# Linformer attention into a hardswish layer: eight first-layer groups by seven products, clips on ScalarE, a new order of steps

## The chip, the cores and the metric

The kernel runs on one core of one Trainium2 chip. The metric is the device time of one execution, in microseconds; the median of three runs before the change is 478.25 us (477.89 to 478.27). Less is better. The engines are called as the profile calls them: PE (matmuls), PEld (its weight loads), DVE (VectorE), ACT (ScalarE), POOL (GpSimd) and SP (SyncE, which here issues DMAs).

## The reference

For each of 8 batches with 8 heads, 1024 positions and head width 64, keys and values are first projected along the sequence to 64 rows; the softmax runs over those 64. The rows of all heads side by side (8192 x 512) go through two layers with a hardswish between them.

```python
k_proj = np.einsum('ks,bhsd->bhkd', E, k)
v_proj = np.einsum('ks,bhsd->bhkd', F, v)
attn = softmax(scale * np.matmul(q, k_proj.transpose(0, 1, 3, 2)))
x = np.matmul(attn, v_proj)          # then (b, s, h*d): 8192 x 512
h = x @ w_in                         # 512 -> 2048
g = h * np.clip(h + 3.0, 0.0, 6.0) / 6.0
out = g @ w_out                      # 2048 -> 512
```

## The kernel before

**Blocks.** A batch is cut into two blocks of 512 tokens (t = 0, 1), so there are 16. Per block the first layer makes `g` as 16 groups of 128 features by 512 tokens; a group L (`first_group`, L578) is 4 steps of depth, each two matmuls of 64 weight columns side by side (`in_columns`, L198 to L200). Its result in PSUM becomes `g` in `h_out` (L573): ACT makes `r = relu(h/6 + 0.5)` (L575), DVE `min(r, 1) * h` (L576).

**Second layer.** It is cut 2 x 2 x 2 and done with seven products instead of eight (the Winograd form of Strassen's method). `Sums` (L662) makes sums of quarters of `g`: `c` (written sc) on POOL, `a` in place and `b` (sb) on DVE, `d` (sd) on POOL in two halves; `a` goes in two calls, one inside the block and a(4,8), groups 4 to 7 with groups 12 to 15, at the start of the next; sums of `w_out` are made once. A `Pair` (L686) is one half of a block's rows: steps 7, 2, 5, 6, 1, 3, 4, each 8 times two matmuls with 256 columns. Products 2 and 5 share a PSUM tile `y`, and 6, 1, 3, 4 share a tile `x`: each adds on top of the last, and after each an engine takes the running value out (ACT by copy, DVE by subtraction), so the next product of the tile waits for that read.

**Four first-layer groups by seven products.** From batch 3 on, the last four groups (12 to 15) are done the same way by a `Quad` (L746): sums of `w_in` are made once (`sums_of_w_in`, L146), and two blocks of `w_in` are changed in place in batch 3 (L930). Four sums of x per block run on POOL (`Quad.sums`, L754). A step is two feature groups by two depths by 256 tokens. Its four results leave by `Quad.out` (L778): for three of them DVE subtracts, ACT makes the relu from SBUF (L784), POOL clips it by 1 (L789) and multiplies (L790); for the fourth, and for all in the very last block, ACT does the relu and DVE clips and multiplies at once (L787). The tiles `m7`, `m2`, `m5` have one buffer each.

**Attention** of the next batch is done beside the blocks. `projected` (L341) is 16 steps of matmuls, copies on ACT, and then two pieces by transposing DMAs on SP. `some_scores` (L349) fills four PSUM tiles for two pairs of heads, which ACT's `exps` free: the first pair's at once, the second's later. `add_up` (L305) sums exponentials on DVE; `sums_turned` (L315) and `spread_sums` (L325) turn and invert the sums on DVE and spread them by two and eight DMAs on SP. `some_values` (L355) fills four PSUM tiles that DVE multiplies into the next `xT` (L301). `load_next` and `behind_that` (L216, L256) load a later batch: POOL waits for the reader of the old data by a copy of one element, then issues the DMAs.

**Order.** Every engine runs its instructions in the order in which they are written. PE's order in a block is a list of steps (`ORDER` L850, `QUADS` L852): L0 is a group, A and B are the two pairs of the block before, N is this block's first pair, Q the quad. `plan` (L863 to L930) hangs acts of the attention on places such as (0, "L1"). `later` is a list of pieces popped one per step; `behind_steps` (L563) puts a piece off by some steps, and `step_done` (L566) counts them. PSUM has eight tiles: four `mm` (groups, and the tiles x) and four `at` (the tiles y, scores, values, projections).

Of the kernel before, what the change touches and what calls it, by code (L numbers as in the profile page):

```python
# [11 lines left out]
ALU = mybir.AluOpType  # L12


@with_exitstack
def kernel(
# [11 lines left out]
    nc = tc.nc  # L28
# [44 lines left out]

    def g_tile():
        return gpool.tile([P, FO, TOK], bf16, tag="g", name="g")
# [8 lines left out]
    ones = consts.tile([P, TOK], bf16, name="ones")  # L84
# [58 lines left out]
    v11, v12, v21, v22 = [w_in_sb[:, k:k + KX, f * P:(f + NQ) * P] for k in (0, KX) for f in (FO - 2 * NQ, FO - NQ)]  # L143
    v_sums = consts.tile([P, 3, KX, NQ * P], bf16, name="v_sums")

    def sums_of_w_in():  # L146
        add(v_sums[:, 0], v11, v21, nc.gpsimd)
        add(v_sums[:, 1], v11, v22, nc.gpsimd)
        sub(v_sums[:, 2], v11, v12, nc.gpsimd)
# [45 lines left out]

# [26 lines left out]

    class Attention:
        def __init__(self, b):
            self.b = b
            self.aT = {}
            self.parts = None
# [17 lines left out]
        def values_out(self, a):  # L245
            nc.scalar.copy(
                self.vp[a * KP:(a + 1) * KP], self.ps[KP:].rearrange("p (h d) -> p h d", d=D))
# [26 lines left out]
        def exps(self, j, tiles, when=lambda f: f()):  # L274
            self.aT[j] = aT = att.tile([P, 2, 2, HT], bf16, tag="aT", name="aT", bufs=KO + 1)
# [20 lines left out]
        def values(self, j, *allocs):  # L296
            return self.quads(lambda r, h: self.vp[r:r + KP, h, :], j, allocs)
# [6 lines left out]

        def add_up(self, *js):  # L305
            if self.parts is None:
                self.parts = att.tile([P, KO, 32], f32, tag="parts", name="parts", bufs=1)
            for j in js:
                nc.vector.tensor_reduce(out=self.parts[:, j], op=ALU.add, axis=mybir.AxisListType.X, apply_transpose=True,  # L309
                                        in_=self.aT[j].rearrange("p a r n -> p (a r n)").rearrange(  # L310
                                            "p (c i) -> p c i", i=32))

        def sums_turned(self):  # L315
            turned, other = [att.tile([P, KO * 32], f32, tag="turned", name="turned", bufs=2) for _ in range(2)]
# [23 lines left out]

# [5 lines left out]

# [47 lines left out]

    class First:
# [131 lines left out]
        def second_scores(self):  # L529
            for j in range(0, KO, 2):  # L530
                aT = att.tile([P, 2, 2, HT], bf16, tag="aT", name="aT", bufs=KO + 1)
# [20 lines left out]
    def h_part(h_ps, xT, t, fo, kos):  # L552
        for ko in kos:
# [19 lines left out]
    def h_out(h_ps, g, fo, when=now):  # L573
        r = rpool.tile([P, TOK], f32, tag="r", name="r")
        nc.scalar.activation(r, h_ps, AF.Relu, bias=0.5, scale=1.0 / 6.0)  # L575
        when(lambda: nc.vector.scalar_tensor_tensor(g[:, fo, :], r, 1.0, h_ps, op0=ALU.min, op1=ALU.mult))  # L576
# [84 lines left out]

    class Sums:  # L662


        def __init__(self, g):
            self.blocks = [g[:, k * KH:(k + 1) * KH, i * HT:(i + 1) * HT] for i in range(2) for k in range(2)]

        def c(self, engine=nc.gpsimd):
            self.sc = spool.tile([P, KH, HT], bf16, tag="sc", name="sc")
            add(self.sc, self.blocks[0], self.blocks[2], engine)  # L670

        def a(self, lo, hi):
            a21, a22 = [x[:, lo:hi] for x in self.blocks[2:]]
            sub(a21, a22, a21)

        def b(self):
            self.sb = spool.tile([P, KH, HT], bf16, tag="sb", name="sb")
            sub(self.sb, self.blocks[0], self.blocks[2])

        def d(self, engine=nc.gpsimd):  # L680
            self.sd = spool.tile([P, KH, HT], bf16, tag="sd", name="sd")
            for lo in range(0, KH, 4):
# [3 lines left out]
    class Pair:  # L686
# [6 lines left out]
        def product(self, n, ps, first=False):  # L693
# [4 lines left out]
                    7: lambda: (a22, w_sums[:, 0])}[n]()  # L698
            for k in range(KH):
# [46 lines left out]
    class Quad:  # L746

        def __init__(self, x, t, g, last):  # L750
            self.g, self.last = g, last
            self.blocks = [x[:, k:k + KX, t, i * HT:(i + 1) * HT] for i in range(2) for k in (0, KX)]

        def sums(self):  # L754
# [7 lines left out]

        def product(self, n, ps, first=False):
            a11, a12, a21, a22 = self.blocks
            x, w = {1: (self.xb, v_sums[:, 1]), 2: (a11, v_sums[:, 2]), 3: (self.xd, v22), 4: (a12, v21),
                    5: (self.xc, v12), 6: (self.xa, v11), 7: (a22, v_sums[:, 0])}[n]
# [6 lines left out]
        def copied(self, name):  # L773
            m = spool.tile([P, TOK], f32, tag="q" + name, name="q" + name)
            nc.scalar.copy(m, self.y)
            return m

        def out(self, h, i, j, engine=None):  # L778
            f = FO - 2 * NQ + j * NQ
            g = self.g[:, f:f + NQ, i * HT:(i + 1) * HT]  # L780

            def relu():
                r = rpool.tile([P, TOK], f32, tag="r", name="r")
                nc.scalar.activation(r, h, AF.Relu, bias=0.5, scale=1.0 / 6.0)  # L784
                r3, h3 = [v.rearrange("p (a n) -> p a n", a=NQ) for v in (r, h)]
                if self.last or engine is nc.vector:
                    behind_steps(1)(lambda: nc.vector.scalar_tensor_tensor(g, r3, 1.0, h3, op0=ALU.min, op1=ALU.mult))  # L787
                else:
                    nc.gpsimd.tensor_scalar(out=r, in0=r, scalar1=1.0, scalar2=None, op0=ALU.min)  # L789
                    nc.gpsimd.tensor_tensor(out=g, in0=r3, in1=h3, op=ALU.mult)  # L790

            behind_steps(2)(relu)

        def step(self, n):
            if n in (7, 2):
                self.y = pat()
            elif n == 6:
                self.x = pmm()
            self.product(n, self.y if n in (7, 2, 5) else self.x, n in (7, 2, 6))
            if n == 7:  # L800
                self.m7 = self.copied("m7")
            elif n == 2:
                self.m2 = self.copied("m2")
            elif n == 5:
                self.m5 = self.copied("m5")
            elif n == 6:
                sub(self.m7, self.m7, self.x)
                self.out(self.m7, 1, 0, nc.gpsimd)
            elif n == 1:
                sub(self.m5, self.m5, self.x)  # L810
                self.out(self.m5, 1, 1, nc.gpsimd)
            elif n == 3:
                sub(self.m2, self.x, self.m2)
                self.out(self.m2, 0, 1, nc.gpsimd)
            else:
                self.out(self.x, 0, 0, nc.vector)
# [15 lines left out]
    for what in "A2 A7 V0 B7 A5 V1 A6 R B2 A1 V2 B5 R A3 B6 V3 A4 B1 R".split():  # L832
# [11 lines left out]
        if what in added:  # L844
# [13 lines left out]
    for b in range(1, B):  # L858
# [18 lines left out]
        def spread(turned, inverted):  # L877
            at(turned, lambda: second.sums_turned())
            at(inverted, lambda: second.spread_sums())

        if b == 1:
            at((0, "B4"), sums_of_w_in)
            at((1, "L0"), add_up(1))
            at((0, "L14"), scores(0, 1))
            at((1, "L1"), scores(2, 3))
            at((1, "N2"), values(0))
            at((0, "L12"), second.load_next)
            at((0, "L14"), add_up(0))
            at((1, "L2"), add_up(2))
            at((1, "L3"), add_up(3))  # L890
            spread((1, "A1"), (1, "B2"))
            at((1, "B4"), values(3))
            at((0, "L6"), second.projected)
            at((1, "B3"), values(1))
            at((1, "B3"), values(2))
            at((1, "B4"), lambda: behind_that(second.recs[1][:1, 0, :1], 3, "q"))
        elif b == 2:
            at((0, "B4"), add_up(2))
            at((0, "B6"), add_up(0))
            at((0, "L0"), second.projected)  # L900
            at((0, "L9"), scores(0, 1))
            at((1, "B4"), values(3))
            at((1, "B1"), values(0))
            at((0, "A1"), second.load_next)
            spread((1, "A1"), (1, "B2"))
            at((0, "L14"), scores(2, 3))
            at((1, "L6"), third.projected)
            at((0, "N5"), add_up(1))
            at((1, "L1"), add_up(3))
            at((1, "L13"), values(2))  # L910
            at((1, "N5"), values(1))
        elif b + 1 < B:
            if b == 3:
                at((0, "start"), second.load_next)
            at((0, "L1"), scores(0, 1))
            at((0, "B7"), add_up(0))
            at((0, "A1"), scores(2, 3), add_up(1))
            at((0, "A3"), add_up(2))
            at((0, "A4"), add_up(3))
            spread((0, "B6"), (0, "B3"))  # L920
            if third:
                at((0, "B4"), lambda: third.projected(pause=False))
                if third.b + 1 < B:
                    at((1, "L7"), third.load_next)
        if 2 < b < B - 1:
            at((1, "L3"), values(0, 1))
            at((1, "L7"), values(2, 3))

        if b == 3:
            at((0, "A6"), lambda: add(v12, v12, v22, nc.gpsimd), lambda: sub(v21, v21, v22, nc.gpsimd))  # L930
# [5 lines left out]
        for t in range(NB):  # L936
# [4 lines left out]
            quads = (b, t) >= (3, 0)  # L941
            if quads:
                pairs["Q"] = Quad(xT, t, g, (b, t) == (B - 1, NB - 1))
            if not start:
                behind[0].sums.a(KH - left, KH)
            left = 2 * NQ if quads else 2
# [73 lines left out]
```

## Time and profile before

| what | value |
|---|---|
| runs | 477.89, 478.25, 478.27 us |
| profiled execution, first to last instruction | span 476.3 us |
| median of the runs less that span | 1.95 us |
| PE busy | 469.6 us, 99% of the span |
| DVE, POOL, ACT busy | 339.4, 306.1, 275.4 us |
| granted clock of PE | 1.000 |

Durations come from the profiled execution. The profile gives its span; its own time with what lies around the span is not listed, so the 1.95 us stand for that. "Busy" counts overlapping instructions once. A row of the page's groups names line, engine, operation, the tiles written and read, how often, then the busy time, the mean of one in ns, and the idle time before. PE's matmuls overlap, so a step's cost is read from the distance to the next step's start. In the waits, a line says who waited for whom, how long in all, how often, and the longest.

### The profile page before, as it was taken

What the parts mean: (1) busy time and instruction counts of PE and PEld (TensorE: products, weight loads), DVE (VectorE), ACT (ScalarE), POOL (GpSimd) and SP (SyncE); (2) the same over time, 40 slices, a digit from 0 to 9 for tenths busy, and PEclk for the clock granted to TensorE, in tenths of its full rate; (3) what the DMA queues carried; (4) which work ended last, traced back from release to release, by engine and by line L of the source; (5) the groups of instructions that cost most, each with busy time, mean ns of one, the idle gap of its engine ahead of it and who ended that gap; (6) DMA issues with size and microseconds to landing.
All of it is one profiled execution on the core that took longest, in us unless ns stands there. A gap on an engine that the chain in (4) does not pass through costs nothing.

```text
span 476.3 us, 14916 instructions
## 1 busy us (share of the span) xinstructions
PE 469.6 (99%) x6428; PEld 346.1 (73%) x6428; DVE 339.4 (71%) x542; ACT 275.4 (58%) x534; POOL 306.1 (64%) x207
## 2 busy tenths in 40 slices
PE   7999999999999999999999999999999999999997
PEld 4554567667677766787787878778687877878797
DVE  2583387688765958886778876887778897747574
ACT  3766478675455654656466565666457545546451
POOL 8634966153335232867897778887788587888820
DMA  9999989688999939996999196962931054111012
GB/s 166 198 200 207 240 146 207 124 144 149 238 180 156 214 100 200 200 206 157 192 165 171 48 228 136 211 126 89 205 101 47 36 125 136 45 47 45 33 59 90
DMA packets 84609, 68.65 MB, mean 144 GB/s; under 512 B 38336, under 2 KB 70592, under 8 KB 84544
## 3 DMA queue, kind: packets, MB, share of 16 engines
q0 software_dynamic: 33024, 29.36, 39.7%
q1 hardware_dynamic: 51152, 37.83, 33.1%
q8 instruction: 50, 0.82, 0.7%
q10 hardware_dynamic: 368, 0.52, 0.3%
q14 instruction: 15, 0.12, 0.1%
HBM read 71.83 MB, written 16.97 MB: 186 GB/s over the span
## 4 chain that ended last, share of the span: by engine, by line
PE 92%; DMA 3%; ACT 2%; POOL 1%; DVE 0%; issue 0%; POOLq 0%
PE mm L200 68%; PE at L200 21%; DMA w_in_sb<-in_moe_w_in_dram 2%; PE at L289 2%; DMA k<-in_k_dram 1%; PE at L268 1%; ACT aT L277 1%; POOL k L110 0%; POOL q L106 0%; PE at L459 0%; DVE parts L309 0%; ACT rec L212 0%; ACT rec L206 0%; ACT m L705 0%; PE at L439 0%
## 5 line engine op out<-in xcount | busy, mean ns | idle before, releaser
L200 PE MATMUL mm<-xT,w_in_sb 128*64 128x512 bf16 (+1 forms) x1808 | 221.8, 375 | 0.2
L576 DVE SCALAR_TENSOR_TENSOR g<-r,mm 128x512 bf16<-128x512 f32 x216 | 146.2, 681 | 70.7 <-ACT r L575 69.8
L575 ACT ACTIVATE r<-mm 128x512 f32<-128x512 f32 x216 | 128.3, 598 | 117.3 <-PE mm L200 111.1
L200 PEld LDWEIGHTS <-w_in_sb 128*64 128x64 bf16 x2048 | 117.0, 110 | 59.7 <-issue 3.3
L200 PEld LDWEIGHTS <-g 128*64 128x64 bf16 x2048 | 112.6, 110 | 24.0 <-issue 4.1
L139 POOL TENSOR_TENSOR sd<-g,sb 128x1024 bf16<-128x1024 bf16 x28 | 59.1, 2130 | 42.0 <-DVE sb L139 40.7
L136 POOL TENSOR_TENSOR sc<-g 128x2048 bf16<-128x2048 bf16 x14 | 57.0, 4072 | 44.7 <-DVE g L576 44.7
L200 PE MATMUL mm<-w_out_sb,g 128*64 128x256 bf16 (+1 forms) x1088 | 77.8, 286 | 0.0
L200 PE MATMUL at<-w_sums,g 128*64 128x256 bf16 x896 | 58.4, 273 | 0.3 <-DVE g L576 0.3
L789 POOL TENSOR_SCALAR r<-r 128x512 f32<-128x512 f32 x27 | 41.5, 1538 | 15.2 <-ACT r L784 15.2
L705 ACT COPY m<-at 128x256 f32<-128x256 f32 x84 | 31.4, 373 | 30.1 <-PE at L200 25.6
L790 POOL TENSOR_TENSOR g<-r,qm 128x512 bf16<-128x512 f32 x27 | 36.3, 1345 | 2.3
L301 DVE TENSOR_TENSOR xT<-at,rec 128x512 bf16<-128x512 f32 x54 | 34.9, 683 | 2.3 <-DMA rec<-turned_rows 1.6
L139 DVE TENSOR_TENSOR o_sb<-m,mm 128x256 f32<-128x256 f32 x60 | 24.8, 413 | 9.6 <-PE mm L200 7.3
L200 PE MATMUL mm<-w_out_sb,sd 128*64 128x256 bf16 x480 | 31.3, 273 | 0.0
L200 PE MATMUL mm<-w_sums,sb 128*64 128x256 bf16 x480 | 31.2, 273 | 0.0
L277 ACT ACTIVATE aT<-at 128x512 bf16<-128x512 f32 x52 | 29.6, 601 | 2.3 <-PE at L268 2.3
L309 DVE TRANSPOSE_TENSOR_REDUCE parts<-aT 128x32 f32<-128x1024 bf16 x24 | 29.7, 1236 | 0.3 <-ACT aT L277 0.3
L200 PEld LDWEIGHTS <-sd 128*64 128x64 bf16 x480 | 26.5, 110 | 3.9 <-issue 0.2
L200 PE MATMUL at<-w_out_sb,sc 128*64 128x256 bf16 x448 | 29.3, 273 | 0.0
L200 PEld LDWEIGHTS <-sc 128*64 128x64 bf16 x480 | 26.5, 110 | 3.8 <-issue 0.3
L200 PEld LDWEIGHTS <-sb 128*64 128x64 bf16 x480 | 26.2, 110 | 4.0 <-issue 1.6
(118 smaller groups left out, 496.3 us busy)
## 6 DMA issues: line engine op xcount, KB each, us to landing
out_dram<-o_sb SPq DMA_DIRECT2D x60, 256.0 KB, 4.2
rec<-turned_rows SPq DMA_DIRECT2D x48, 256.0 KB, 6.1
k<-in_k_dram POOLq DMA_DIRECT2D x7, 1024.0 KB, 11.4
v<-in_v_dram POOLq DMA_DIRECT2D x7, 1024.0 KB, 15.9
q<-in_q_dram POOLq DMA_DIRECT2D x7, 1024.0 KB, 21.0
w_in_sb<-in_moe_w_in_dram POOLq DMA_DIRECT2D x7, 256.0 KB, 9.9
w_out_sb<-in_moe_w_out_dram POOLq DMA_DIRECT2D x3, 512.0 KB, 14.2
k<-in_k_dram POOLq DMA_DIRECT2D x4, 256.0 KB, 6.0
```

The costliest lines, as they stand in the source:

```text
L136: engine.tensor_tensor(out=out, in0=x, in1=y, op=ALU.add)
L139: engine.tensor_tensor(out=out, in0=x, in1=y, op=ALU.subtract)
L200: nc.tensor.matmul(ps[lo:lo + width], stationary[:, lo:lo + width], moving, **flags)
L277: when(lambda r=r: nc.scalar.activation(aT[:, :, r, :], tiles[r].rearrange("p (a n) -> p a n", a=2), AF.Exp, scale=scale))
L289: nc.tensor.matmul(tiles[t][c:c + D], stationary(r, 2 * j + a), self.weights(j, a)[r:r + KP], start=True, stop=True)
L301: when(lambda t=t: nc.vector.tensor_mul(self.xT[:, j, t, :], av[t], rec[:, t]))
L309: nc.vector.tensor_reduce(out=self.parts[:, j], op=ALU.add, axis=mybir.AxisListType.X, apply_transpose=True, in_=self.aT[j].rearrange("p a ...
L575: nc.scalar.activation(r, h_ps, AF.Relu, bias=0.5, scale=1.0 / 6.0)
L576: when(lambda: nc.vector.scalar_tensor_tensor(g[:, fo, :], r, 1.0, h_ps, op0=ALU.min, op1=ALU.mult))
L705: self.copy(m, ps)
L789: nc.gpsimd.tensor_scalar(out=r, in0=r, scalar1=1.0, scalar2=None, op0=ALU.min)
L790: nc.gpsimd.tensor_tensor(out=g, in0=r3, in1=h3, op=ALU.mult)
```

## The change

Eight groups instead of four, 8 to 15, are done by seven products, as two quads: Q for groups 12 to 15 and R for 8 to 11. The list of steps is written anew, the sums `a` to `d` and the sums of x (`+a`, `+b`, `+c`, `+d`, `+x`) become entries of it, and the last batch has lists of its own. The sums of x are made once for both quads. The clip on POOL goes: ACT makes two relus, `relu(0.5 - h/6)` and of that `relu(1 - r)`, and POOL only multiplies. The relu of a quad's result still stands two steps behind, DVE's product three steps behind instead of one, and the product of a group one step behind. The plan of acts is a table; several acts are at other places. The tile `aT` has four buffers instead of five, and `ones` is narrower. The code also keeps records of what is written when, which issue no instruction.

```diff
-    QUADS = ("L0 A7 L1 A6 L2 B7 L3 A1 L4 B2 L5 A3 L6 B5 L7 A4 "
-             "L8 Q7 Q2 B6 L9 Q6 N2 Q5 B1 L10 Q1 B3 L11 Q3 N5 B4 Q4").split()
+ORDER_OF_QUADS = ('L0 R7 A7 L1 +b +x L2 L3 L4 +d L5 L6 B2 A6 R2 R6 L7 R5 B7 B5 A1 +c R1 Q7 B6 A3 R3 Q6 B1 A4 '
+                  'Q2 B3 N2 Q5 Q1 N5 +a R4 Q3 B4 Q4')
+ORDER_OF_LAST = (('R7 L0 +b +x L1 R2 L2 A7 A6 L3 L4 +d L5 L6 B2 R6 L7 R5 B7 B5 +c A1 Q7 R1 B6 A3 R3 Q6 B1 A4 '
+                  'Q2 B3 N2 Q5 Q1 N5 +a R4 Q3 B4 Q4'),
+                 ('L0 R7 +x A7 +b L1 L2 R2 L3 L4 L5 L6 B2 R6 A6 L7 R5 +d A1 B7 B5 Q7 R1 +c B6 A3 R3 Q6 B1 A4 '
+                  'Q2 B3 N2 Q5 Q1 N5 +a R4 Q3 B4 Q4'))
-    ORDER = ("L0 A7 L1 A6 L2 B7 L3 A1 L4 B2 L5 A3 L6 B5 L7 A4 "
-             "L8 L9 B6 L10 N2 L11 B1 L12 N5 L13 B3 L14 L15 B4").split()
+ORDER_OF_L = ('L0 A7 L1 A6 L2 B7 L3 A1 L4 L5 B2 A3 L6 B5 L7 A4 L8 L9 B6 L10 N2 B1 L11 L12 N5 L13 B3 L14 '
+              'L15 B4')
...
+PLANS = {
+    1: ('0.L6:P 0.L12:l 0.L14:S01,u0 0.B4:wQ,wR 1.L0:u1 1.L1:S23 1.L2:u2 1.L3:u3 1.A1:T 1.B2:I '
+        '1.B1:V0 1.B3:V1,V2 1.B4:V3,q'),
+    2: ('0.B4:u2 0.B6:u0 0.L0:P 0.L9:S01 1.B4:V3 1.B1:V0 0.L2:l 1.A1:T 1.B2:I 0.L14:S23 1.B2:p '
+        '0.N5:u1 1.B7:u3 1.B3:V2 1.N5:V1'),
+    3: ('0.L1:S01 0.Q2:u0 0.L5:S23,u1 0.B5:u2 0.A1:u3 0.Q2:T 0.N2:I 0.B4:p 1.Q1:m 1.L3:V01 1.B1:V23 '
+        '0.L3:l 0.L1:iR 0.L3:iQ'),
+    4: ('0.L1:S01 0.Q2:u0 0.L5:S23,u1 0.B5:u2 0.A1:u3 0.Q2:T 0.N2:I 0.B4:p 1.Q1:m 1.L3:V01 1.B1:V23'),
+}
+FIRST_QUADS = (3, 0)
+RELU_BEHIND = 2
+PRODUCT_BEHIND = 3
+L_BEHIND = 1
+LEFT = 4
...
+    quarters = {"Q": Quarter(FO - 2 * NQ), "R": Quarter(FO - 4 * NQ)}
...
-                nc.scalar.activation(r, h, AF.Relu, bias=0.5, scale=1.0 / 6.0)
...
-                    nc.gpsimd.tensor_scalar(out=r, in0=r, scalar1=1.0, scalar2=None, op0=ALU.min)
+                    nc.scalar.activation(r, h, AF.Relu, bias=0.5, scale=-1.0 / 6.0)
+                    nc.scalar.activation(r, r, AF.Relu, bias=1.0, scale=-1.0)
                     nc.gpsimd.tensor_tensor(out=g, in0=r3, in1=h3, op=ALU.mult)
```

In the table, S is `some_scores`, V `some_values`, u `add_up`, T `sums_turned`, I `spread_sums`, P and p `projected` of the next batch and the one after, l and m their `load_next`, q a load of queries, w the sums of `w_in` for a quad and i its in-place sums. Plan 4 holds for batches 4 to 6. Before, in batches 3 to 6, S01 stood at L1, u0 at B7, S23 and u1 at A1, u2 at A3, u3 at A4, T at B6, I at B3 and p at B4 of t=0; V01 stood at L3, V23 and m at L7 of t=1.

More of the change, by code (lines that the diff above doesn't have):

```diff
@@ L71, in pat, with wrote, there @@
         return ps_at.tile([P, TOK], f32, tag="at", name="at")
+    written = {}
     def g_tile():
-        return gpool.tile([P, FO, TOK], bf16, tag="g", name="g")
+        g = gpool.tile([P, FO, TOK], bf16, tag="g", name="g")
+        written[id(g)] = set()
+        return g
+    def wrote(g, i, fos):
+        written[id(g)].update((i, f) for f in fos)
+    def there(g, i, fos):
+        assert all((i, f) in written[id(g)] for f in fos), (i, fos)
     scratch = g_tile().rearrange("p f n -> p (f n)")
@@ L83 @@
     nc.vector.memset(wide, 1.0)
-    ones = consts.tile([P, TOK], bf16, name="ones")
+    ones = consts.tile([P, D], bf16, name="ones")
     nc.vector.memset(ones, 1.0)
@@ L142, with __init__, sums, in_place @@
     NQ, KX = 2, KO // 2
[L143 to L149, printed above, removed]
+    class Quarter:
+        def __init__(self, f):
+            self.f, self.summed, self.changed = f, False, False
+            self.v11, self.v12, self.v21, self.v22 = [
+                w_in_sb[:, k:k + KX, a * P:(a + NQ) * P] for k in (0, KX) for a in (f, f + NQ)]
+            self.v_sums = consts.tile([P, 3, KX, NQ * P], bf16, name="v_sums%d" % f)
+        def sums(self):
+            assert not self.summed
+            self.summed = True
+            add(self.v_sums[:, 0], self.v11, self.v21, nc.gpsimd)
+            add(self.v_sums[:, 1], self.v11, self.v22, nc.gpsimd)
+            sub(self.v_sums[:, 2], self.v11, self.v12, nc.gpsimd)
+        def in_place(self):
+            assert self.summed and not self.changed
+            self.changed = True
+            add(self.v12, self.v12, self.v22, nc.gpsimd)
+            sub(self.v21, self.v21, self.v22, nc.gpsimd)
+    quarters = {"Q": Quarter(FO - 2 * NQ), "R": Quarter(FO - 4 * NQ)}
     def sums_of_w_out():
@@ L245, in values_out @@
         def values_out(self, a):
+            self.halves.add(a)
             nc.scalar.copy(
@@ L552, in h_part @@
     def h_part(h_ps, xT, t, fo, kos):
+        assert not any(q.changed and q.f <= fo < q.f + 2 * NQ for q in quarters.values())
         for ko in kos:
@@ L575, in h_out, with product @@
         nc.scalar.activation(r, h_ps, AF.Relu, bias=0.5, scale=1.0 / 6.0)
-        when(lambda: nc.vector.scalar_tensor_tensor(g[:, fo, :], r, 1.0, h_ps, op0=ALU.min, op1=ALU.mult))
+        def product():
+            nc.vector.scalar_tensor_tensor(g[:, fo, :], r, 1.0, h_ps, op0=ALU.min, op1=ALU.mult)
+            for i in range(2):
+                wrote(g, i, [fo])
+        when(product)
     def first_group(xT, t, g, fo, when=now):
@@ L669, in c @@
             self.sc = spool.tile([P, KH, HT], bf16, tag="sc", name="sc")
+            for i in range(2):
+                there(self.g, i, range(KH))
+            assert not self.ready
             add(self.sc, self.blocks[0], self.blocks[2], engine)
@@ L875, in add_up @@
             return lambda: second.add_up(*js)
[L877 to L930, printed above, removed]
+        acts = {"P": lambda: second.projected(), "p": lambda: third and third.projected(pause=b < 3),
+                "l": lambda: second.load_next(), "m": lambda: third and third.b + 1 < B and third.load_next(),
+                "T": lambda: second.sums_turned(), "I": lambda: second.spread_sums(),
+                "q": lambda: behind_that(second.recs[1][:1, 0, :1], 3, "q")}
@@ new lines, in act @@
+        def act(what):
+            if what in acts:
+                return acts[what]
+            if what[0] == "w":
+                return quarters[what[1]].sums
+            if what[0] == "i":
+                return quarters[what[1]].in_place
+            return {"S": scores, "V": values, "u": add_up}[what[0]](*map(int, what[1:]))
+        for entry in PLANS.get(b, PLANS[4] if 3 < b < B - 1 else "").split():
+            t, place, what = entry.replace(":", ".").split(".")
+            at((int(t), place), *map(act, what.split(",")))
```

110 lines of the change are left out of this document (73 added, 37 removed).

## The prediction

> **What bounds the kernel now.** I read the page's busy shares first, then the waits, then the busy time of two blocks, then PE's timeline inside them.
>
> ```profile
> span 476.3 us, 14916 instructions
> ...
> PE 469.6 (99%) x6428; PEld 346.1 (73%) x6428; DVE 339.4 (71%) x542; ACT 275.4 (58%) x534; POOL 306.1 (64%) x207
> ```
>
> PE leads by far. The view of waits must say whether it works or waits:
>
> ```profile
> PE at L200 <- DVE g L576: 0.3, 1, 0.3
> ```
>
> In the products of both layers (line 200) PE waits for another engine once, for 0.3 us, while ACT's relus wait for PE 158 times, 111.1 us in all. Now two blocks of batch 5 (t=0 and t=1, from the start of L0 to the start of the next L0):
>
> ```profile
> 301.14:330.00 28.86, 28.86 (x428) 22.61 (x426) 23.88 (x36) 17.82 (x37) 23.03 (x15) 1.00 0.64 131
> 330.00:356.99 26.99, 26.99 (x396) 21.12 (x394) 19.77 (x33) 15.45 (x31) 20.49 (x13) 1.00 0.79 162
> ```
>
> Columns: stretch and length, then PE, PEld, DVE, ACT, POOL, the granted clock (1.00). PE is busy for all of it, so no stall is there to be removed. Time can come only from PE having less to do, and is lost by every new PE wait.
>
> **What the change is worth on PE.** PE's timeline in that stretch prices each step by the distance to the next start:
>
> ```profile
> 306.18 1.04 PE L200 MATMUL at<-w_sums,g 128*64 128x256 bf16 x16
> 307.05 1.03 PE L200 MATMUL mm<-xT,w_in_sb 128*64 128x512 bf16 x8
> 307.91 1.04 PE L200 MATMUL mm<-w_sums,sb 128*64 128x256 bf16 x16
> ...
> 319.89 0.60 PE L200 MATMUL mm<-xa,w_in_sb 128*64 128x256 bf16 x8
> 320.32 1.04 PE L200 MATMUL at<-w_sums,g 128*64 128x256 bf16 x16
> ```
>
> A pair's product takes 307.05 - 306.18 = 0.87 us, a group L 0.865, a seven-product step (Q6) 0.434. Four groups cost 4 x 0.865 = 3.46, the seven products in their place 7 x 0.434 = 3.04: 0.42 less per block. The row of x sums counts 10 blocks (xc x10), the ones from batch 3 on: **10 x 0.42 = 4.2 us** less PE work. Attention, pairs and tail keep their PE work.
>
> A rule speaks against this. The Trainium skill, "TensorE: Matmul & The Clock Gate", Back-to-back issue gap, says that in a stream of weight loads and matmuls the spacing is set by both, some 81 ns per matmul at 128 columns and 131 at 512. An estimate on a line between gives 98 at 256, so 56 x 98 - 32 x 131 ns = 1.3 us more per block. The trace disagrees: 8 matmuls of 256 columns in 0.434 us are 54 ns each, 8 of 512 in 0.865 are 108. I keep the rows; rival 4 holds the rest.
>
> **What the other engines get, per block.** The rows:
>
> ```profile
> L576 DVE SCALAR_TENSOR_TENSOR g<-r,mm 128x512 bf16<-128x512 f32 x216 | 146.2, 681 | 70.7 <-ACT r L575 69.8
> ...
> L789 POOL TENSOR_SCALAR r<-r 128x512 f32<-128x512 f32 x27 | 41.5, 1538 | 15.2 <-ACT r L784 15.2
> ...
> L784 ACT ACTIVATE r<-qm 128x512 f32<-128x512 f32 x30 | 19.0, 633 | 9.2 <-DVE qm L139 9.2
> ```
>
> - DVE: minus four L products (0.681), plus three subs (0.688) and one product (0.688): +0.03.
> - POOL: minus three clips (1.538), plus three products (1.345, L790's row): -0.6.
> - ACT: minus four relus (0.598), plus three copies (0.586), nine relus from SBUF (0.633) and one from PSUM (0.597): +5.7. It gets 23.5 of 28.4 us in t=0, 21.1 of 26.6 in t=1. The second relu reads the first's result; the trace has no such pair. Bounds for two: 2 x 0.49 (distance of two relus that follow at once) to 2 x 0.633 plus a gap; I take 1.2.
>
> No engine passes PE's sum. What decides is lateness inside the block.
>
> **A walk through block t=0** (batches 3 to 6), time 0 at L0, PE without stalls. Ends on PE: L1 3.0, scores 0 and 1 3.6, L5 7.1, scores 2 and 3 7.6, R6 11.1, L7 12.0, A1 15.0, R3 18.1, Q6 18.5, B1 19.4, Q2 20.7, B3 21.6, Q5 22.9, Q1 23.3, N5 24.2, R4 24.6, Q3 25.1, B4 25.9, projection 27.7, Q4 28.1.
>
> ACT, in written order: Q3's two relus (1.2) and Q4's one (0.5) of the block before end at 1.7; then, at 0.49 per 512 columns and 0.25 per 256, L0, R7's copy, A7's copy, L1, two exps, L2, exp, L3, exp: the last frees its score tile at 6.6, before scores 2 and 3 (7.1). It is level with PE by L7 (relu to 12.5; R6's two behind it to 13.7). POOL: x sums from 2.6, when Q3's product of the block before ends, 4 x 1.16 and, between them, DVE's sb (1.2): 8.4; sd 2 x 2.13: 12.7 (A3 needs it at 16.8); R6's product 13.7 to 15.0; sc 4.07: 19.0 (N5 needs it at 23.3); then R1 to 20.3, R3 to 21.6, Q6 to 22.9. Three places are tight:
>
> 1. Q2's copy on ACT (the one tile m2) waits for R3's product, 21.6, so ends at 22.2; Q5, at 22.4, adds into the same PSUM tile. Margin 0.2.
> 2. Q3 (24.6) adds into the tile that Q1's sub on DVE reads. DVE before it: Q6's and B1's subs to 19.8, add_up(0) (1.236) to 21.0, then sums_turned, B3's sub, the reciprocal (0.94), Q1's sub. Without contention sums_turned takes 0.30 + 2 x 0.22 + 2 x 0.28 = 1.3 and the sub ends at 24.1; with a wait of 0.4 for the rest of R3's product, 24.6: margin about 0.
> 3. In t=1, B2 at 7.9 needs a PSUM slot that DVE's first value product frees; before it DVE has Q4's product (to 1.7), a(4,8), L0, L1, sb (to 6.0), L2 and L3 (to 7.2), so 7.9. Margin 0.
>
> The lock is seen in these rows:
>
> ```profile
> 304.00 1.28 POOL L790 TENSOR_TENSOR g<-r,qm 128x512 bf16<-128x512 f32 x1
> ...
> 304.11 2.25 DVE L139 TENSOR_TENSOR sb<-g 128x2048 bf16<-128x2048 bf16 x1
> ...
> 317.21 4.07 POOL L136 TENSOR_TENSOR sc<-g 128x2048 bf16<-128x2048 bf16 x1 [1.78 <-DVE g L576]
> ...
> 319.91 1.45 DVE L321 COPY turned<-turned 32x128 f32<-32x128 f32 x1
> ```
>
> The copy (0.22 alone) ends at 321.36, just after sc (321.28); sb takes 2.25 where it takes 1.23 beside an idle POOL. The Trainium skill, "SBUF — State Buffer", Who interferes with whom, says the same: a DVE copy, or a DVE operation with two SBUF inputs, and a GpSimd operation block each other whole. By that rule the adds of sums_turned wait too; that is rival 2.
>
> The last batch has no attention beside it, its last block every product on DVE; the tail's first steps find a(4,8) as late as now (2.2 us after Q4, needed at 2.6): 0. In batches 1 and 2 L5 goes ahead of B2, value products and add_ups move by a few steps, and two quarters' sums take 3.5 us more of a POOL that then idles 9.4 us: 0, bounds -0.3 and +0.5. In batch 3 the second quarter's in-place sums add 2.3 us to POOL ahead of sd, which has 4 to spare. load_next goes from L7 to Q1 of t=1: mark and three issues, 0.2 + 2.7 us of POOL, now stand ahead of Q1's product; that ends at 26.9 of 26.3, and the next A7 starts 1.3 into its block: 0.7 left. Its loads (11 to 21 us to landing) have over 25 us. spread_sums goes from B3 to N2: SP issues two and eight DMAs from 24 on (7 us now), 6.1 us to landing, while the first value product comes 9 us later: 0.
>
> So the place costs: each of the tight ones between 0 and 1.25; I charge 0.1 in each of the eight blocks with attention. **Sum: -4.2 + 0.8 = -3.4.** The profiled execution's span becomes 476.3 - 3.4 = 472.9; the median of the runs stands 1.95 above the span, for what lies around it, which the change leaves: 478.25 - 3.4 = **474.8**.
>
> **Rivals.**
> 1. As forecast, 473.8 (place costs and batches 1 and 2 at their best) to 476.4: 60%. For: every step is at a row's price. Against: margins of 0 to 0.2.
> 2. sums_turned is blocked twice: POOL takes the lock after the first copy for Q6's product, and add, second copy and all behind come 1.3 later; Q1's sub ends at 25.9 and Q3 waits 1.25. In two to four of the blocks t=0 that is 2.5 to 5.0 more: 477.3 to 479.8. For: the rows of the lock. Against: the adds' rows (0.28) show no wait so far. 20%.
> 3. **Slower:** POOL's queue is late in every block: sc (4.07) stands ahead of R1, R3 and Q6, so if R6's product or sd ends a microsecond later, Q2's copy, Q5 and the end of the block go with it. Nine blocks have POOL products; at 0.75 each it is 6.8, so 480.8. It decides from 0.47 per block (4.2 / 9), when sc starts after 15.7. For: R6's two relus stand behind L7's on ACT. Against: POOL has 0.6 less to do. 14%.
> 4. The change doesn't do what it says: 56 weight loads where there were 32 (110 ns each, PEld up from 73%) eat the saved columns: 478.25 + 0.8 = 479.0. Against: Q6's 0.434. By the page's rule it would be 13 us more, 491; 2 of this rival's 6%.
>
> **How the numbers follow.** The measurement can tell about 0.2% (0.96 us) from no change. Faster: rival 1's 60, 8 of rival 2, 2 of rival 3: 70%. Same: 8, 2 and 4 of rival 4: 14%. Slower: 4, 10 and 2: 16%. The range runs from 473.8 to 478.9, and leaves out the end of rival 2 and nearly all of rival 3, some 19%. The likeliest case's own range is 473.8 to 476.4.
>
> **What would show it.** Right: 40 L groups gone (x1728 to x1408 matmuls), products at 0.434, two blocks together near 55.0 us instead of 55.85, PE without gaps. Wrong at place 1: PE waits for ACT's qm copy before Q5. At place 2: PE idle before Q3 with DVE qm named and long turned rows. Rival 3: the copy of m2 waits for POOL g in every block, t=1 too. Rival 4: a Q step above 0.45 us. I am wrong if PE shows more than 3 us of new waits that none of these places holds.

## The result, and the profile after

The changed kernel takes 483.87 us (median of four runs, 483.5 to 487.03) where the kernel before takes 478.1 on the same chip: ratio 1.0133 [1.0103, 1.0162]. It is 1.3% slower. One of the four runs, the one of 487.03 us, had a granted clock of 0.993; by the medians alone the loss is 1.2%. The prediction said 474.8 and put 478.9 as its upper end, so it missed the direction too. The profiled run took 483.7 us, with a span of 481.9; the span before was 476.3, so the step to explain is +5.6 us.

The page of the changed kernel, its span and busy shares:

```profile
span 481.9 us, 15515 instructions
...
PE 467.6 (97%) x6668; PEld 361.4 (75%) x6668; DVE 343.6 (71%) x545; ACT 320.0 (66%) x618; POOL 310.8 (64%) x212
```

PE was busy for 99% of the span and is now busy for 97%: it has less to do in a longer time. The view of waits, three of PE's lines in the two layers (who waits for whom, total, times, longest):

```profile
PE mm L251 <- DVE qm L176: 3.4, 4, 1.0
PE mm L251 <- DVE g L628: 1.8, 3, 0.6
...
PE at L251 <- ACT qm L848: 0.8, 1, 0.8
```

Before there was one such line, of 0.3 us; one of that size is there after too. (Line 251 is the old line 200, 628 the old 576, 176 the old 139; 373, 374 and 379 are the old 321, 322 and 327.) Batch 5, cut at the starts of L0, in the columns used for it before:

```profile
304.86:334.23 29.37, 28.59 (x452) 23.84 (x450) 24.16 (x36) 23.76 (x48) 22.57 (x15) 1.00 0.75 143
334.23:362.15 27.92, 27.16 (x421) 22.71 (x419) 20.08 (x33) 19.27 (x38) 19.80 (x13) 1.00 0.64 152
```

The batch takes 57.29 us where it took 55.89 by the same cuts (301.15 to 357.04), and the length of each half is now above PE's busy time: 0.78 and 0.76 us of hard idle time, at an undisturbed clock.

The steps themselves cost what was foreseen. PE's timeline of the changed kernel in batch 4:

```profile
265.49 0.60 PE L251 MATMUL mm<-xd,w_in_sb 128*64 128x256 bf16 x8
265.93 0.60 PE L251 MATMUL mm<-xa,w_in_sb 128*64 128x256 bf16 x8
266.36 1.04 PE L251 MATMUL mm<-w_sums,sb 128*64 128x256 bf16 x16
```

Two steps of a quad take 0.44 and 0.43 us, start to start. So some 4.2 us of PE work did go. PE's busy time, down by only 2.0 us, is no measure of it: the run with one quad below, which has the PE work of the kernel before, shows 473.1 us of it against 469.6. Against the 4.2 stand 9.7 us of waits from batch 3 on, where the kernel before has 0.5: -4.2 + 9.2 is 5.0, beside 5.6; the other 0.6 was not traced. Where they lie, from the starts of PE's steps against the time that their columns take: before Q3 in t=0, 1.19 in batch 3 and 0.95 in each of batches 4 to 6 (4.0); in t=1 of batches 3 to 5, 0.77 before L6 and 0.31 before B2 (3.2), and 0.2 before B2 in batch 6; before Q5 in batch 3, 0.97; the last 1.3 is in pieces of at most 0.22, mostly 0.15 before Q4. By length, batch 3 gains 2.60 us, batches 4 and 5 some 1.4 each, batch 6 0.67, and the rest changes by less than 0.4 each.

**Before Q3** (place 2). The timeline of batch 4, t=0, of all engines; the row of POOL counts three products, and the bracket on PE's row is its wait:

```profile
267.13 3.75 POOL L870 TENSOR_TENSOR g<-r,qm 128x512 bf16<-128x512 f32 x3
...
269.40 0.33 DVE L373 COPY turned<-turned 32x128 f32<-32x128 f32 x1
...
269.77 1.26 DVE L374 TENSOR_TENSOR inv<-turned 32x128 f32<-32x128 f32 x1
...
271.04 0.22 DVE L373 COPY turned<-turned 32x128 f32<-32x128 f32 x1
...
271.95 0.93 DVE L379 RECIPROCAL inv<-inv 64x128 f32<-64x128 f32 x1
...
272.81 0.62 DVE L176 TENSOR_TENSOR qm<-qm,mm 128x512 f32<-128x512 f32 x1
...
273.48 0.63 PE L251 MATMUL mm<-xd,w_in_sb 128*64 128x256 bf16 x8 [0.79 <-DVE qm L176]
```

Q1's product left PE at about 271.4. Its subtraction starts at 272.81, because DVE has `sums_turned` and the reciprocal in front of it, and the first add of `sums_turned` takes 1.26 us where it takes 0.28: it ends 0.15 us after POOL's row does (270.88). Such a hold of a DVE instruction by one of POOL's is called the lock here. Q3 needs the tile at 272.5 and gets it at 273.48.

**Before L6 and B2** (place 3). Batch 4, t=1, whose L0 starts at 276.95:

```profile
280.90 1.64 ACT L625 ACTIVATE r<-mm 128x512 f32<-128x512 f32 x3
281.54 0.69 DVE L628 SCALAR_TENSOR_TENSOR g<-r,mm 128x512 bf16<-128x512 f32 x1 [1.23 <-ACT r L625]
...
282.04 1.15 POOL L176 TENSOR_TENSOR xd<-xT,xb 128x512 bf16<-128x512 bf16 x1
282.14 2.13 DVE L176 TENSOR_TENSOR sb<-g 128x2048 bf16<-128x2048 bf16 x1
...
284.19 1.27 DVE L628 SCALAR_TENSOR_TENSOR g<-r,mm 128x512 bf16<-128x512 f32 x2
...
284.92 1.05 PE L251 MATMUL mm<-xT,w_in_sb 128*64 128x512 bf16 x8 [0.60 <-DVE g L628]
285.39 0.68 DVE L353 TENSOR_TENSOR xT<-at,rec 128x512 bf16<-128x512 f32 x1
...
286.12 1.06 PE L251 MATMUL at<-w_sums,g 128*64 128x256 bf16 x16
```

ACT comes late to L1's relu, DVE idles for 1.23 us and then begins sb, which takes 2.13 instead of 1.23 because POOL's last sum of x runs beside its start. The products of L2 and L3 wait behind sb with two PSUM tiles in their hands, so L6 finds none; and B2's tile comes free only after the multiplication at 285.39.

**Before Q5** (place 1), in batch 3 alone, where POOL has the loads and the in-place sums of `w_in` besides:

```profile
209.64 3.72 POOL L870 TENSOR_TENSOR g<-r,qm 128x512 bf16<-128x512 f32 x3
...
210.95 2.50 DVE L373 COPY turned<-turned 32x128 f32<-32x128 f32 x1
...
212.17 0.58 ACT L848 COPY qm<-at 128x512 f32<-128x512 f32 x1 [1.03 <-POOL g L870]
...
212.81 0.63 PE L251 MATMUL at<-xc,w_in_sb 128*64 128x256 bf16 x8 [0.81 <-ACT qm L848]
```

ACT's copy waits for R3's product and Q5 for the copy. The DVE row is met again below.

### The profile page after: what moved, and what is told of

Same layout as the page of the kernel before. It is cut to its first block, busy times and chain, and to the rows that moved or that the text cites. A ratio compares the mean times of both kernels' runs of the same rounds, so it can differ in the third digit from the quotient of the medians.

```text
span 481.9 us, 15515 instructions
## 1 busy us (share of the span) xinstructions
PE 467.6 (97%) x6668; PEld 361.4 (75%) x6668; DVE 343.6 (71%) x545; ACT 320.0 (66%) x618; POOL 310.8 (64%) x212
## 4 chain that ended last, share of the span: by engine, by line
PE 82%; DVE 8%; ACT 5%; issue 3%; DMA 1%; POOL 0%; DVEq 0%; POOLq 0%
PE mm L251 57%; PE at L251 20%; PE at L340 1%; DMA k<-in_k_dram 1%; PE at L319 1%; DVE parts L361 1%; DVE qm L176 1%; DVE g L628 1%; ACT aT L328 1%; DVE turned L373 1%; DVE inv L374 1%; DVE inv L379 1%; ACT r L625 1%; ACT vp L297 1%; DVE o_sb L176 1%
## 5 line engine op out<-in xcount | busy, mean ns | idle before, releaser
L251 PE MATMUL mm<-xT,w_in_sb 128*64 128x512 bf16 (+1 forms) x1568 | 180.5, 369 | 1.9 <-DVE g L628 1.8
L251 PEld LDWEIGHTS <-w_in_sb 128*64 128x64 bf16 x2048 | 119.5, 110 | 66.0 <-issue 14.1
L628 DVE SCALAR_TENSOR_TENSOR g<-r,mm 128x512 bf16<-128x512 f32 x176 | 117.1, 680 | 47.5 <-ACT r L625 46.8
L625 ACT ACTIVATE r<-mm 128x512 f32<-128x512 f32 x176 | 103.8, 600 | 65.7 <-PE mm L251 63.0
L870 POOL TENSOR_TENSOR g<-r,qm 128x512 bf16<-128x512 f32 x54 | 68.1, 1276 | 48.8 <-ACT r L869 37.1
L868 ACT ACTIVATE r<-qm 128x512 f32<-128x512 f32 x54 | 34.0, 629 | 14.1 <-DVE qm L176 14.0
L848 ACT COPY qm<-at 128x512 f32<-128x512 f32 x60 | 35.0, 583 | 12.5 <-PE at L251 7.6
L869 ACT ACTIVATE r<-r 128x512 f32<-128x512 f32 x54 | 34.0, 630 | 1.7
L176 DVE TENSOR_TENSOR qm<-qm,mm 128x512 f32<-128x512 f32 x40 | 26.9, 673 | 8.6 <-ACT qm L848 4.1
```

What stands on the lines that cost most here:

```text
L176: engine.tensor_tensor(out=out, in0=x, in1=y, op=ALU.subtract)
L251: nc.tensor.matmul(ps[lo:lo + width], stationary[:, lo:lo + width], moving, **flags)
L848: nc.scalar.copy(m, ps)
L868: nc.scalar.activation(r, h, AF.Relu, bias=0.5, scale=-1.0 / 6.0)
L869: nc.scalar.activation(r, r, AF.Relu, bias=1.0, scale=-1.0)
```

## The experiments

The working theory was that three independent causes share the waits: the reciprocal and the lock before Q3, sb ahead of the value products in t=1, and POOL's queue in batch 3. The main rival was that the work of the second quad (ACT's double relus, POOL's products) fills the engines, whatever the order. All edits are to the changed kernel unless said otherwise. The kernel before measured 478.2 to 478.6 us beside them.

### One act moved at a time

**sums_turned and the reciprocal behind Q1**, so that Q1's subtraction comes first:

```diff
-0.Q2:T 0.N2:I
+0.Q1:T,I
```

> The changed kernel, with sums_turned and spread_sums of batches 3 to 6 moved from Q2 and N2 to behind Q1, where POOL is idle for some 4 us. Theory (DVE's turn of the sums is blocked by POOL's products and holds up Q1's sub, so PE waits 0.95 us before Q3 in each of four blocks t=0): these waits go, 483.8 - 3.8 = 480.0, within 0.6. Rival (ACT has too much to do with two relus for each clip, and every wait is a late relu): the waits stay, 483.5 to 484.

Measured 487.5 us, ratio 1.0172 [1.0142, 1.0203]: a miss. The waits before Q3 are gone, as foreseen, and larger ones stand before Q4: 1.2 us in batches 3 to 5 and 2.9 in batch 6 (2.73 of it shown as idle). Q3's own subtraction now stands behind everything that was moved, and behind `a`. DVE in batch 4:

```profile
273.15 0.21 DVE L373 COPY turned<-turned 32x128 f32<-32x128 f32 x1
273.40 0.28 DVE L374 TENSOR_TENSOR inv<-turned 32x128 f32<-32x128 f32 x1
...
274.27 0.94 DVE L379 RECIPROCAL inv<-inv 64x128 f32<-64x128 f32 x1
275.14 1.51 DVE L176 TENSOR_TENSOR g<-g 128x1024 bf16<-128x1024 bf16 x1
276.57 0.67 DVE L176 TENSOR_TENSOR qm<-mm,qm 128x512 f32<-128x512 f32 x1
```

The last row is the subtraction that Q4 waits for. The first two show what `sums_turned` costs when POOL has no row beside it: 0.21 and 0.28. In batches 3 to 5 the projection's matmuls (1.7 us) hide part of the queue; batch 6 has no projection.

**b behind L3**, so that the products of L2 and L3 and the first value product are not behind it:

```diff
-L0 R7 A7 L1 +b +x L2 L3 L4 +d
+L0 R7 A7 L1 +x L2 L3 +b L4 +d
```

> The changed kernel, with +b moved from behind L1 to behind L3 in the list of quads, so that DVE makes the products of L2 and L3 and the first value product before sb. Theory (sb, stretched to 2.1 us by POOL's sums of x, stands ahead of the products that free the PSUM slots for L6 and B2 in t=1): PE's waits before L6 (0.88) and B2 (0.42) go in three blocks, 483.8 - 3.9 = 479.9, within 0.7. Rival (the slots are late because ACT's relus are late): L6 still waits 0.5 or more, 482 to 483.8.

Measured 481.15 us, ratio 1.0054 [1.0039, 1.0068]. The waits before L6 and B2 are gone, sb takes 1.22 us there and meets no POOL row; the waits before Q3 stay (1.20 and three of 0.95). The time is 0.5 us above the theory's range: the expectation's 0.88 and 0.42 were too high, as the waits before L6 and B2 are 0.77 and 0.31, 3.2 in three blocks instead of 3.9. The move gave 2.7 of them.

**Both:**

> Both moves together. Theory: the two waits are independent and add up, 483.8 - 7.7 = 476.1, within 0.8, so below the 478.1 of the kernel before. Rival (PE then waits for something else that comes 1 us later, since ACT, DVE and POOL are all nearly full): half of it or less, 479.5 or more.

Measured 486.46 us, 1.0153 [1.0135, 1.0171]. That is far above the theory's 476.1, and the two do not add up: the spans would give 485.8 + 478.9 - 481.9 = 482.8 us, and this run has 484.5. The first one's loss before Q4 stays, and in t=1 of batches 3 to 5, where the waits before L6 and B2 are gone, R2 now waits 0.56 us and Q5 0.25, as the rival had it.

**add_up(0) earlier**, which takes 1.24 us out of DVE's queue ahead of `sums_turned`:

```diff
-0.Q2:u0
+0.R6:u0
```

> The changed kernel, with add_up(0) moved from Q2 to behind R6, where DVE is idle, so that sums_turned starts 1.2 us earlier but in the same company: three products on POOL without a gap. Theory (the copies and adds of sums_turned are kept out until POOL's row of products ends): sums_turned ends at most 0.4 us earlier and Q3 still waits 0.6 or more in each of four blocks, 482.2 to 483.8. Rival (DVE's queue is merely 1 us too long there, whatever POOL does): the waits go, 480.0.

Measured 483.47 us, 1.0093 [1.0072, 1.0115], so almost nothing against 483.87, and inside the theory's 482.2 to 483.8. `sums_turned` starts 0.8 us sooner and loses most of it again: the wait before Q3 falls from 0.95 to 0.70 us in batches 4 to 6. DVE in batch 4 of this run:

```profile
268.60 0.38 DVE L373 COPY turned<-turned 32x128 f32<-32x128 f32 x1
269.01 1.27 DVE L374 TENSOR_TENSOR inv<-turned 32x128 f32<-32x128 f32 x1
270.29 1.21 DVE L373 COPY turned<-turned 32x128 f32<-32x128 f32 x1
```

Two of its four small instructions are now held for a product of POOL's row each, instead of one. That is the lock: a shorter queue would have brought the whole 0.8.

### Who pays: the order or the second quad

**The new order with one quad**: groups 8 to 11 are computed as groups again, where R's seven steps stood.

```diff
-L0 R7 A7 ... B2 A6 R2 R6 L7 R5 B7 B5 A1 +c R1 Q7 B6 A3 R3 Q6 ... N5 +a R4 Q3 B4 Q4
+L0 L8 A7 ... B2 A6 L9 L7 L10 B7 B5 A1 +c L11 Q7 B6 A3 Q6 ... N5 +a Q3 B4 Q4
```

> The changed kernel's new order and plan, but groups 8 to 11 as groups again (L8 to L11 stand where R's seven steps stood, 4 x 0.865 us on PE instead of 7 x 0.434): the order alone, without the second quad. PE's work is that of the kernel before. My theory: the waits of t=1 (first relus behind the sum b on DVE, 1.3 us in each of batches 3 to 5) belong to the order and stay, 3.9 us; the waits before Q3 come from sums_turned meeting POOL's row of products of both quads, and with R's products gone they mostly go (0 to 1 us left). So 478.5 + 3.9 + 0.5 = 482.9 us (482.0 to 483.8). Rival A: all new waits come with the second quad's work on ACT and POOL: 478.5 (477.9 to 479.2). Rival B: the order alone makes the waits before Q3 too: 486.5 (485.5 to 487.5).

Measured 487.13 us, 1.0182 [1.0168, 1.0196]. Rival B's 486.5 is met, and my theory fell: I had given the waits before Q3 to the row of products of two quads, and they are there with one. Batch 4 of this run:

```profile
269.49 0.68 DVE L373 COPY turned<-turned 32x128 f32<-32x128 f32 x1
...
271.41 0.93 DVE L379 RECIPROCAL inv<-inv 64x128 f32<-64x128 f32 x1
...
272.26 0.62 DVE L176 TENSOR_TENSOR qm<-qm,mm 128x512 f32<-128x512 f32 x1
...
272.94 0.63 PE L251 MATMUL mm<-xd,w_in_sb 128*64 128x256 bf16 x8 [0.64 <-DVE qm L176]
```

The lock takes 0.46 here (0.68 against 0.22) instead of 1.0, but R4, which gave Q3 0.43 us more time, is not there either. What both kernels share is the reciprocal right in front of the subtraction, with little between Q1 and Q3. So the spans split the result: the new order with one quad costs 485.4 - 476.3 = 9.1 us, and the second quad within it brings 485.4 - 481.9 = 3.5 us back, of the 4.2 foreseen. The main rival, that the second quad's work makes the waits whatever the order, is out as the main cause. The waits of the two runs, 9.1 and 9.7 us, are not all the same ones, though: with one quad those before L6 are only 0.27, and 0.25 before Q3 in each t=1 of batches 3 to 6 and 1.8 before groups of batch 7 are its own.

**The reciprocal alone moved**, from N2 to Q1, with `sums_turned` left where it is:

```diff
-0.Q2:T 0.N2:I
+0.Q2:T 0.Q1:I
```

> The changed kernel with one edit: the reciprocal and the spreading stand behind Q1 instead of N2 (b stays behind L1, a in front of Q3). It tells what the reciprocal's place ahead of Q1's subtraction is worth by itself. My theory: sums_turned is still held up 1.0 us by POOL's row of products, but Q1's subtraction then ends before Q3 wants its tile, so the four waits of some 1.0 before Q3 go; a (1.5) and the reciprocal (0.94) then stand ahead of Q3's subtraction, which B4 and the projection hide in batches 3 to 5 but not in batch 6 (1.5 there). The waits in t=1 stay (3.9). 483.87 - 4.0 + 1.7 = 481.5 us (480.8 to 482.3), ratio 1.007. Rival: the lock alone sets Q3's lateness, and moving the reciprocal changes nothing: 483.9.

Measured 480.98 us, 1.0055 [1.0042, 1.0067], inside the theory's 480.8 to 482.3. DVE in batch 4 of this run:

```profile
269.07 1.26 DVE L374 TENSOR_TENSOR inv<-turned 32x128 f32<-32x128 f32 x1
...
271.26 0.68 DVE L176 TENSOR_TENSOR qm<-qm,mm 128x512 f32<-128x512 f32 x1
271.85 0.94 DVE L379 RECIPROCAL inv<-inv 64x128 f32<-64x128 f32 x1
```

The waits before Q3 are down to 0.15 in batches 4 to 6, though the lock is untouched (the add still takes 1.26 us); 0.39 stays in batch 3. So with two quads the lock is not enough by itself: 1.0 of lock and 0.93 of reciprocal together make 0.95 of lateness, and taking away the reciprocal ends it. Taking away the lock alone was not run; that it would end the wait too is an estimate from these sizes, 0.98 against 0.95. In batch 6 Q4 now waits 0.66, less than the 1.5 I expected.

**Two relus instead of a clip, in the kernel before:**

```diff
-relu(h/6 + 0.5) on ACT, min(r, 1) on POOL
+relu(0.5 - h/6) and relu(1 - r) on ACT
```

> The kernel before with nothing changed but the clip: two relus on ACT instead of relu and POOL's clip, four groups by seven products, old order. Theory (ACT has room, POOL's queue gets shorter): no difference, 478.1 within 0.5. Rival (0.63 us more per result on ACT delays the copies and relus behind it): 479 or more.

Measured 478.4 us, 0.9996 [0.9984, 1.0009]: no difference, with ACT's busy time up from 275.4 to 289.5 and POOL's down from 306.1 to 262.2.

**The clip back on POOL, in the changed kernel:**

> The changed kernel with one relu on ACT and the clip on POOL again. My theory (waits come from DVE's queue and the lock with POOL; ACT's 5.7 us more are hidden): POOL gets 9 blocks x 6 x 1.54 us more, some 30 us of work in blocks of 26 to 28, and becomes the bound: 495 to 515. Rival (ACT's second relus are what holds PE up): 478 to 483.

Measured 534.97 us, 1.1184 [1.1155, 1.1213], even more than the theory's 495 to 515. The view of waits of this run:

```profile
PE at L251 <- ACT qm L848: 39.5, 9, 5.6
```

and of ACT's own waits:

```profile
ACT qm L848 <- POOL g L870: 57.4, 17, 6.7
```

With 54 clips of 1.49 us on it, POOL is late with its products, ACT's copies wait for their tiles and PE, before Q5 of all nine blocks, for the copies, as in rival 3 of the prediction; so in this order the second quad needs the relus on ACT. PE's granted clock was 0.954 over this run, so part of the loss is the clock.

### Towards a version without the new waits

**b behind L3, and the projection at N5**, so that its 1.7 us lie between Q1 and Q3:

```diff
-L1 +b +x L2 L3 L4          0.B4:p
+L1 +x L2 L3 +b L4          0.N5:p
```

> Run e2 (+b behind L3) with the projection of the batch after next moved from B4 to N5, so that PE has 1.7 us of other work between Q1 and Q3 in the blocks t=0 of batches 3 to 5; DVE's order is unchanged. Theory (Q3 waits for Q1's sub, which DVE makes 0.95 us late): the wait goes in three blocks (1.2, 0.95, 0.95), stays in batch 6, which has no projection: 481.15 - 3.1 = 478.1, within 0.6. Rival (as in e1 a wait of the same size turns up one step later, at Q4): 481.

Measured 482.72 us, 1.0087 [1.0059, 1.0115], above the theory's 478.1 and the rival's 481. Q3 no longer waits in batches 3 to 5, but in t=1 other steps do (0.3 to 0.8 each): ACT's copies of the projection now stand ahead of the relus there.

**The same, with the reciprocal behind Q1 and `a` behind Q3:**

> Run e5 with spread_sums moved from N2 to behind Q1, and +a from behind N5 to behind Q3, so that on DVE the reciprocal (0.93) and a (0.7) no longer stand ahead of the subs of Q1 and Q3. Theory: batch 6 loses most of its 0.95 too, the other blocks nothing: 0.7 less than e5, about 477.4. Rival (the sums come to SP's DMAs 1 us later, and the value products of t=1 wait for them): 0.5 or more above e5.

Measured 480.12 us, 1.0037 [1.0026, 1.0048]: 2.6 us less than the run before it, but not the theory's 477.4. What stays is mostly 0.65 to 0.73 us before R2 in t=1 of batches 3 to 5, where DVE's second multiplication of `xT` is late behind sb.

**The same, with the projection left at B4** (the diff is against the version with b behind L3):

```diff
-0.N2:I                  N5 +a R4 Q3 B4 Q4
+0.Q1:I                  N5 R4 Q3 +a B4 Q4
```

> The changed kernel with b behind L3 (as in the experiment that moved it), the spreading of the inverse sums behind Q1 instead of N2, and the in-place sum a behind Q3 instead of in front of it; the projection stays at B4. PE has nothing less to do than in the changed kernel. My theory: Q1's subtraction no longer stands behind the reciprocal, so the four waits before Q3 go (1.0 us each, 4.0 from the 481.15 of the run with b moved alone), and Q4, which has B4 and the projection (2.6 us) to cover Q3's subtraction, waits in batch 6 at most. That gives 477.2 us (476.6 to 478.0), ratio to the kernel before 0.997. The waits before R2 in t=1 (0.65 each) that the run with the projection at N5 had are there from the projection's copies on ACT and should be gone. Rival: they come from a being late on DVE, and stay with a behind Q3: 4 x 0.65 more, 479.8 (479.2 to 480.4).

Measured 477.71 us, 0.9992 [0.9983, 1.0001], inside the theory's 476.6 to 478.0 and 0.5 above its middle; the rival's 479.8 is out. Batch 4 again:

```profile
267.74 1.26 DVE L374 TENSOR_TENSOR inv<-turned 32x128 f32<-32x128 f32 x1
...
269.92 0.68 DVE L176 TENSOR_TENSOR qm<-qm,mm 128x512 f32<-128x512 f32 x1
...
270.51 0.94 DVE L379 RECIPROCAL inv<-inv 64x128 f32<-64x128 f32 x1
...
270.65 0.63 PE L251 MATMUL mm<-xd,w_in_sb 128*64 128x256 bf16 x8
```

The add is still held to the end of POOL's row, the subtraction goes ahead of the reciprocal, and PE's row has no wait above 0.15.

**One edit more, batch 3's in-place sums of Q ahead of the sums of x:**

```diff
-0.L1:iR 0.L3:iQ
+0.L1:iR,iQ
```

> The kernel with b behind L3, the spreading behind Q1 and a behind Q3 (477.71 us), with one edit more: the in-place sums of Q's quarter of w_in (2.06 + 1.15 us on POOL) stand ahead of the sums of x in batch 3, not behind them and the loads, so that they fall into a stretch in which POOL waits 4.69 us for xT. My theory: in batch 3 everything behind on POOL, sc and R3's product too, comes some 1 us sooner, Q2's copy on ACT with it, and the waits before Q5 (0.89) and Q3 (0.40) of that batch go: 476.6 us (476.2 to 477.2), ratio 0.997. Rival: the in-place sums must wait for the last group of batch 2 (to 188.8) and only push the sums of x and sd out, so that sc starts at most 0.3 sooner: 477.5 (477.2 to 478.0).

Measured 477.33 us, 0.9974 [0.9957, 0.999]: 0.3% under the kernel before, with an interval that ends just below 1, which no other version has. In batch 3 the waits before Q5 (0.89) and Q3 (0.40) are gone, as the theory said, but the time lies in the rival's range (477.2 to 478.0) and not in the theory's, and the span of 475.8 us is no shorter than the 475.7 without this edit. Two waits came at the batch's start, 0.46 in the step of a group and 0.42 in R7. DVE there in this run:

```profile
188.13 1.82 DVE L176 TENSOR_TENSOR g<-g 128x1536 bf16<-128x1536 bf16 x1
189.87 1.27 DVE L628 SCALAR_TENSOR_TENSOR g<-r,mm 128x512 bf16<-128x512 f32 x2
```

The in-place sum of `g` took 0.94 us without the edit. It now meets POOL's sums of `w_in` (from 187.98 on), and the products of groups and the multiplications of `xT` behind it come 0.9 us later. The edit took away one such meeting of DVE and POOL and made another, so it is not shown to bring anything by itself.

## Why the prediction was wrong

1. **What bounds the kernel: right.** PE's work sets the end and each new wait adds to it.
2. **The term of PE: right.** A step of a quad costs 0.434 to 0.44, and with the waits taken out, batch 4 of the version with three moves takes 55.34 us against 55.90 before (from the first value product of t=1 to that of the next batch). That is 0.55 of the 0.84 foreseen; 0.29 of the rest are waits of 0.14 before Q3 in t=0 and 0.15 before Q4 in t=1, for a subtraction on DVE. Rival 4 is refuted: the second quad brought 3.5 us in the new order.
3. **The terms of ACT and POOL: right in size, partly wrong in effect.** The pair of relus costs 1.3 us (630 and 629 ns on average) instead of 1.2, and in the kernel before it costs nothing, as the experiment shows. But in t=1 ACT comes late to L1's relu (280.90, where PE's step began at 279.13 and took 0.87), behind R7's and A7's copies and two casts of the projection, and the 1.23 us that DVE idles there feed place 3.
4. **The three places: found, and priced wrongly.** The walk named each of them, though at place 3 only B2 and not L6, which waits for products in the same queue on DVE. The step that failed is the sentence "I charge 0.1 in each of the eight blocks". Measured: 0.95 to 1.19 at place 2 in four blocks, 1.1 at place 3 in three (0.77 of it before L6) and 0.2 in a fourth, 0.97 at place 1 in one; 0.8 us in the sum stood for 8.4.
 - At place 2 the walk took 0.4 for the lock and let Q1's subtraction end at 24.1 to 24.6; rival 2 had the add held by Q6's product and 25.9, and got 20%. The add was held 0.98, and the subtraction ended at 25.85 (272.81 + 0.62 after the block's start at 247.58). The view of before that spoke for it was the 1.45-us copy in my own fence; I called the adds free of it because their rows in the kernel before were 0.28; but there POOL was idle from 321.28 to 323.69, and they met no row of it.
 - At place 3 the walk took sb at 1.2, though the fence two paragraphs on showed it at 2.25 beside POOL. It took 2.13. With ACT's lateness, L3's product ended 8.5 us after L0 instead of 7.2.
 - The places were treated as small chances that average out. This program does the same in like batches: before Q3 the wait is 0.95 in batches 4, 5 and 6; at place 3 it is 1.1 in 3, 4 and 5, and 0.2 only in batch 6, which has no projection. A margin of 0 charged at a tenth fits neither case.
5. **The rivals.** Rival 2 came as it was written, and place 2 alone would give 478.25 - 4.2 + 4.0 = 478.05, inside its 477.3 to 479.8. I had set the rivals against one another, and places 2 and 3 came together. Rival 3, late in every block, is seen only in batch 3; the chain sc, R1, R3, Q6 on POOL kept its time elsewhere.
6. **The sign by which I would be wrong**, more than 3 us of new waits that none of the places holds, comes only if the waits before L6 (2.3 us), which place 3 did not name, are counted as outside it: with the 1.3 of small pieces that is 3.6. All else is in the three places.

On the lock, the Trainium skill, "SBUF — State Buffer", Who interferes with whom, calls the port pair that DVE and GpSimd share an exclusive lock, and says that a DVE instruction with two SBUF inputs contends with a GpSimd instruction that reads SBUF. The trace agrees for the adds (1.26 us beside the row, 0.28 without it). In batch 3 a copy took 2.50 us beside two products.

## What to carry to other kernels

When PE is full, price a new order of steps by what stands in front of each read that frees a PSUM tile, on the engine that does the read, with the contended durations of the rows (1.26 for a 0.28-us add, 2.13 for a 1.23-us sum), not with the free ones. A margin near 0 in a block that repeats came whole or hardly at all here: work it out for both, and let several such places be late at once. Put what nobody waits for soon (here a reciprocal, a sum for the next block) behind such a read, and check what then stands behind it.

## What was not expected of the hardware

- The 0.22-us copy of batch 3 took 2.50 us: it began at 210.95, in the second of three products on POOL (a row of 3.72 us from 209.64, 1.24 each), and ended at 213.45, with the row (213.36). It was not let in between the second and the third product. In batch 4 and in the run with add_up earlier, single small instructions were held for about one product each.
- After the 2.73 us in which PE idled in batch 6 of the first experiment, the clock was halved for 3.4 us, from 391.6 us on. PE's row after the wait, and the stretch by windows (the third-last number of the second line is the granted clock):

```profile
392.32 2.77 PE L251 MATMUL mm<-xT,w_in_sb 128*64 128x256 bf16 x16 [2.73 <-DVE qm L176]
```

```profile
391.62:395.04 3.42, 2.71 (x18) 1.91 (x19) 2.17 (x5) 1.75 (x3) 1.36 (x2) 0.50 0.32 90
```

  These 16 matmuls (Q4 and L0) take 1.49 us in the same kind of row elsewhere, so a wait of 2.7 costs over a microsecond more than itself; waits of up to 1.2 us left the clock alone. The Trainium skill, "TensorE: Matmul & The Clock Gate", HAM oscillation — how this bites in real kernels, gives idle gaps above some 3.4 us as those to avoid; here 2.73 was enough.
